# 103 unread TensorE passes in ten shapes behind the last store of a fused dynamic-convolution and squared-ReLU feed-forward kernel

## The chip, the cores and the metric

One Trainium2 chip, one of its cores. The metric is device microseconds of that core. Beside the plain times there is one profiled execution, whose span is the time from the first to the last recorded instruction.

## What is computed

The kernel computes a dynamic convolution (a softmax over 7 taps weighs the last 7 rows, for 8 heads) and feeds the result to a feed-forward block with a squared ReLU.

```python
batch, seq, d_model = (8, 4096, 192); n_heads, K = 8, 7
w = softmax(weight_gen, axis=-1)                       # [B, S, H, K]
x_unf = x_pad[:, s + k, :].reshape(B, S, K, H, D // H) # 7 shifted rows
a = np.einsum('bshk,bskhg->bshg', w, x_unf).reshape(B * S, D)
h = a @ w_in                                           # [32768, 192] @ [192, 2048]
r = np.maximum(h, 0.0)
return ((r * r) @ w_out).astype(np.float32)            # [2048, 192]
```

The change adds nothing to this: the outputs are stored before the added passes in program order, and the passes write PSUM tiles that nothing reads.

## The kernel before, in words

The 32768 rows are cut into 64 chunks of 512 (`N`). For each chunk VectorE and ScalarE make the convolution, and TensorE makes both products. Each operand of a product is split into a high and a low part in the type `F32R`; a product of such operands is one pass per call, while a product in plain `F32` gives two matmul records per call (the 9 calls at L567 show as 18).

Most passes go in pairs over half of the array's rows. `mm1` (L430) and `mm2_turned` (L503) call the matmul twice, once with partitions 0 to 63 and once with 64 to 127 (`rows = slice(h * D1, (h + 1) * D1)`, `D1 = 64`), each with a stationary operand of 128 columns and 512 moving columns, into two different PSUM banks. Every pass has a weight load of its own (`LDWEIGHTS`, listed as the engine PEld).

The last chunk (`c = NCH - 1`) has another form. `mm2` and `mm2_tile` (L476) use all 128 rows: per step one pass of 384 columns with the high part `gh` and one of 192 with the low part `gl`. The last quarter of its columns is finished in four passes into `acc` (L767) and eight passes of 192 columns into the PSUM tile `rest` (L770). VectorE adds `rest` to `tmp` (L773), and `store` (L557) issues the last output transfer on SyncE's queue. That is the last line of the kernel's body.

The schedule is written by hand: each engine runs its instructions in program order, and waits are placed where a tile's readers and writers are on different engines. Two pools of PSUM hold one bank per tile: `ps_h` with four buffers of the name `ph` in turn, and `ps_o` with `acc0` to `acc3`. At the end `rest` and `acc3` are the banks still read; the other three `ph` buffers and `acc0` to `acc2` are the six that the change takes. `ghs[NCH - 1, NF - 1]` is the high part of the last 128 hidden units of the last chunk (128 x 512), and `V` holds the second product's weights (128 x 16 x 384), both `F32R` and both resident until the end.

Of the kernel before, what the change touches and what calls it, by code (L numbers as in the profile page):

```python
# [8 lines left out]
F32 = mybir.dt.float32  # L9
# [12 lines left out]
def kernel(  # L22
# [531 lines left out]
    def store(c, t0, t1):  # L554
        o_sb, _ = outs[c]
        tsl = slice(t0, t1)
        nc.sync.dma_start(out=out_v[:, rows_of(c) + t0:rows_of(c) + t1, :], in_=o_sb[:, tsl])  # L557
# [215 lines left out]
    nc.vector.tensor_tensor(out=o_sb[:, t], in0=rest[:, 0:D], in1=tmp[:, t, 0:D], op=ALU.add)  # L773
    store(c, t, TC)


# [1 line left out]
_INS = ["x", "weight_gen", "moe_w_in", "moe_w_out"]  # L778
# [26 lines left out]
```

## Time and profile before

| what | value |
|---|---|
| time, median of 2 runs | 2231.13 us (2231.03 to 2231.23) |
| the profiled execution's span | 2229.4 us |
| TensorE matmul (PE) busy | 2224.8 us, 100% of the span |
| weight loads (PEld) busy | 1846.2 us, 83% |
| VectorE, ScalarE, GpSimd busy | 1869.8, 1805.4, 9.9 us |

Busy shares are unions of overlapping records: two passes of a pair that run side by side count once, and the end of a pass is modelled, so the spacing of the starts says more than the length of a record. The time from one start to the next is called the spacing below. The time outside the span (2231.13 against 2229.4) is 1.7 us.

### The profile page before, as it was taken

Reading aid. Unit: us, or ns where it says so; the run is one execution under the profiler, and the core shown is the slowest. Engines: PE = TensorE matmul, PEld = TensorE weight load, DVE = VectorE, ACT = ScalarE, POOL = GpSimd, SP = SyncE. Lnnn points to the kernel's source line nnn. Section 1 sums busy time; section 2 is a strip of 40 time slices with the busy share of each in tenths; the row PEclk is TensorE's granted clock in tenths of the full one; section 3 lists DMA queues with packets and bytes.
Section 4 is the critical chain, followed back from the end, with each engine's and each line's share of the span. In section 5 each row is a group of like instructions: output and inputs, shape, how many; then the busy total and the mean of one; then the engine's idle time right before and its main releaser. Section 6 shows DMA issues by size and latency. Waiting matters only on the chain.

```text
span 2229.4 us, 50051 instructions
## 1 busy us (share of the span) xinstructions
PE 2224.8 (100%) x19486; PEld 1846.2 (83%) x19486; DVE 1869.8 (84%) x2866; ACT 1805.4 (81%) x3492; POOL 9.9 (0%) x18
## 2 busy tenths in 40 slices
PE   9999999999999999999999999999999999999999
PEld 8888888888888888888888888888888888888888
DVE  9888888888888888888898888888888888888885
ACT  8888888888888888888888888888888888888886
POOL 0000000000000000000000000000000000000000
PEclk9999999999999999999999999999999999999999
DMA  8433323333233333333332333323333233332322
GB/s 221 96 85 92 90 59 100 83 94 99 57 92 89 88 100 75 74 95 82 100 85 64 100 85 92 88 60 100 84 94 96 54 98 86 91 100 66 82 60 53
DMA packets 323117, 195.30 MB, mean 88 GB/s; under 512 B 223944, under 2 KB 281288, under 8 KB 319040
## 3 DMA queue, kind: packets, MB, share of 16 engines
q1 hardware_dynamic: 321584, 188.58, 33.8%
q0 software_dynamic: 1296, 3.54, 0.9%
q8 instruction: 152, 2.49, 0.5%
q14 instruction: 85, 0.70, 0.1%
HBM read 106.39 MB, written 49.55 MB: 70 GB/s over the span
## 4 chain that ended last, share of the span: by engine, by line
PE 100%; POOL 0%; DVE 0%; issue 0%; POOLq 0%
PE acc L503 50%; PE ph L430 46%; PE acc L467 1%; PE acc L476 1%; PE acc L430 0%; PE acc L341 0%; PE acc L567 0%; PE ph L329 0%; PE ph L770 0%; PE acc L329 0%; PE acc L767 0%; DVE o_sb L773 0%; POOL ident masks.py:199 0%; POOL ident masks.py:197 0%; POOL ex L92 0%
## 5 line engine op out<-in xcount | busy, mean ns | idle before, releaser
L503 PE MATMUL acc<-gh,V 64*128 64x512 f32 x5952 | 1007.4, 386 | 0.0
L430 PE MATMUL ph<-xh,W 64*128 64x512 f32 x6084 | 853.9, 386 | 0.0
L447 ACT ACTIVATE rg<-ph 128x512 f32<-128x512 f32 x992 | 539.1, 597 | 351.5 <-PE ph L430 351.4
L503 PE MATMUL acc<-gl,V 64*128 64x512 f32 x3968 | 772.4, 386 | 0.0
L459 DVE TENSOR_TENSOR gl<-rg,gh 128x512 fp32r<-128x512 f32 x1008 | 644.4, 678 | 139.0 <-ACT gh L455 137.4
L430 PEld LDWEIGHTS ph<-xh,W 64*128 64x128 f32 x6084 | 569.6, 184 | 120.4 <-ACT rg L445 0.4
L503 PEld LDWEIGHTS acc<-gh,V 64*128 64x128 f32 x5952 | 557.5, 184 | 117.1
L451 ACT ACTIVATE rg<-rg 128x512 f32<-128x512 f32 x1008 | 581.3, 633 | 0.2
L455 ACT CAST gh<-rg 128x512 fp32r<-128x512 f32 x1008 | 576.1, 626 | 3.2 <-PE acc L476 3.2
L503 PEld LDWEIGHTS acc<-gl,V 64*128 64x128 f32 x3968 | 371.7, 184 | 78.0
L430 PE MATMUL ph<-xl,W 64*128 64x512 f32 x3042 | 427.3, 386 | 0.0
L266 DVE TENSOR_TENSOR pr<-xt,wt 128x768 f32<-128x768 f32 (+1 forms) x441 | 411.7, 946 | 2.3
L279 DVE TENSOR_TENSOR pr<-pr 128x768 f32<-128x768 f32 x366 | 347.0, 948 | 0.1
L430 PEld LDWEIGHTS ph<-xl,W 64*128 64x128 f32 x3042 | 284.9, 184 | 59.9
L310 DVE TENSOR_TENSOR xl<-xT,xh 128x512 fp32r<-128x512 f32 x186 | 117.7, 688 | 180.9 <-ACT xh L307 180.9
L307 ACT CAST xh<-xT 128x512 fp32r<-128x512 f32 x186 | 102.7, 624 | 0.1
L513 DVE TENSOR_TENSOR raw<-acc,raw 128x512 f32<-128x512 f32 x124 | 79.9, 686 | 5.9 <-ACT raw L511 5.9
L511 ACT COPY raw<-acc 128x512 f32<-128x512 f32 x124 | 66.6, 597 | 0.0
L237 ACT ACTIVATE wt<-wt 128x224 f32<-128x224 f32 x62 | 24.3, 392 | 47.4 <-DVE wt L236 47.4
L393 DVE STREAM_TRANSPOSE xr<-pr 128x768 f32<-128x768 f32 x62 | 60.6, 978 | 2.1
L525 DVE STREAM_TRANSPOSE raw<-raw 64x512 f32<-64x512 f32 x62 | 43.6, 704 | 2.1
L522 DVE STREAM_TRANSPOSE raw<-raw 128x512 f32<-128x512 f32 x62 | 43.7, 704 | 0.0
(93 smaller groups left out, 449.8 us busy)
## 6 DMA issues: line engine op xcount, KB each, us to landing
xT<-xd SPq DMA_DIRECT2D x124, 384.0 KB, 5.0
xt<-in_x_dram SPq DMA_DIRECT2D x30, 1344.0 KB, 6.9
out_dram<-o_sb SPq DMA_DIRECT2D x63, 384.0 KB, 2.7
xd<-xr SPq DMA_DIRECT2D x248, 96.0 KB, 2.0
o_sb<-raw SPq DMA_DIRECT2D x1488, 16.0 KB, 1.8
raw<-raw SPq DMA_DIRECT2D x62, 128.0 KB, 4.2
wt<-in_weight_gen_dram SPq DMA_DIRECT2D x31, 224.0 KB, 3.2
raw<-in_moe_w_in_dram SPq DMA_DIRECT2D x16, 192.0 KB, 5.3
```

Of the source, the lines that this page charges most:

```text
L266: tt(out=dst, in0=src, in1=wf[:, t0 * H:t1 * H, k:k + 1].broadcast_to([P, m, G]), op=ALU.mult)
L279: tt(out=prs[k0], in0=prs[k0], in1=prs.pop(k), op=ALU.add)
L307: nc.scalar.copy(parts["h"][:, k, n], src[k][:, n])
L310: tt(out=parts["l"][:, k, n], in0=src[k][:, n], in1=parts["h"][:, k, n].bitcast(F32), op=ALU.subtract)
L430: nc.tensor.matmul(two[i], w, xx[rows, k], start=(n == 0), stop=(n == len(seq) - 1))
L447: nc.scalar.activation(r, ph, AF.Relu)
L451: nc.scalar.activation(r, r, AF.Square)
L455: nc.scalar.copy(gh, rgs[c, fb])
L459: nc.vector.tensor_tensor(out=gl, in0=rgs.pop((c, fb)), in1=ghs[c, fb].bitcast(F32), op=ALU.subtract)
L503: nc.tensor.matmul(accs[c][b + h], w, g[rows], **fl)
L511: nc.scalar.copy(X[:, k], acc[b])
L513: nc.vector.tensor_tensor(out=X[:, k], in0=acc[b + 1], in1=X[:, k], op=ALU.add)
```

## The change

Behind the last `store` 103 passes are added, all with moving data `mv = ghs[NCH - 1, NF - 1]` and stationary columns of `V`, each with `start=True, stop=True`. None is read. `bk[0]` to `bk[2]` are the three free `ph` tiles, `bk[3]` to `bk[5]` new tiles `acc0` to `acc2`. Nothing else is touched.

```diff
     store(c, t, TC)
 
+    h0, h1 = slice(0, D1), slice(D1, P)
+    mv = ghs[NCH - 1, NF - 1]
+    bk = [ps_h.tile([P, N], F32, name="ph") for _ in range(3)] + [ps_o.tile([P, N], F32, name=f"acc{t}") for t in range(3)]
+
+    def run(items):
+        for b, rows, m, n0, n1, f in items:
+            nc.tensor.matmul(bk[b][0:m, n0:n1], V[rows, f, 0:m], mv[rows, n0:n1], start=True, stop=True)
+
+    allr = slice(0, P)
+    run((0, allr, P, 0, N, f) for f in range(8))
+    run((h + 1, r, P, 0, N, f) for f in range(6) for h, r in enumerate((h0, h1)))
+    run((3, h0, P, 0, N, f) for f in range(6))
+    run((h + 1, r, P, 0, N // 2, f) for f in range(6) for h, r in enumerate((h0, h1)))
+    run((h + 4, r, 96, 0, N, f) for f in range(6) for h, r in enumerate((h0, h1)))
+    run((h + 1, r, P, 0, N, f + g) for f in (0, 2, 4) for h, r in enumerate((h0, h1)) for g in range(2))
+    for g in range(3):
+        run([(3, allr, P, 0, N, g)])
+        run((h + 4, r, P, 0, N, g) for h, r in enumerate((h0, h1)))
+    run((0, allr, 96, 0, N, f) for f in range(6))
+    run((0, allr, P, 0, N - P, f) for f in range(6))
+    run((b, slice(Q * b, Q * b + Q), P, 0, N, f) for f in range(5) for b in range(4))
```

The ten groups in the order in which they run (Q is 32):

| group | passes | rows | moving columns | stationary columns |
|---|---|---|---|---|
| A | 8 | all 128 | 512 | 128 |
| B | 12 | halves in turn | 512 | 128 |
| C | 6 | the lower half alone | 512 | 128 |
| D | 12 | halves in turn | 256 | 128 |
| E | 12 | halves in turn | 512 | 96 |
| F | 12 | lower, lower, upper, upper | 512 | 128 |
| G | 9 | all, lower, upper, three times | 512 | 128 |
| H | 6 | all 128 | 512 | 96 |
| I | 6 | all 128 | 384 | 128 |
| J | 20 | the four quarters of 32 in turn | 512 | 128 |

## Rows read from the trace of the kernel before

**Rows 1.** The page: span, and busy time of the engines.
```profile
span 2229.4 us, 50051 instructions
PE 2224.8 (100%) x19486; PEld 1846.2 (83%) x19486; DVE 1869.8 (84%) x2866; ACT 1805.4 (81%) x3492; POOL 9.9 (0%) x18
```

**Rows 2.** Chain that ended last, from 2205 us: start, length, engine, tile, line.
```profile
2224.86 0.42 PE acc L767 x4
2225.28 0.91 PE ph L770 x8
2226.19 0.02 issue
2226.21 0.36 DVE o_sb L773
```

**Rows 3.** Timeline of the end: start, length, engine, line, operation, shape, count.
```profile
2225.12 0.27 PE L770 MATMUL ph<-V,gh 128*128 128x192 f32 x1
...
2225.25 0.42 DVE L552 TENSOR_TENSOR o_sb<-acc,raw 128x128 f32<-128x128 f32 x2 [0.71 <-ACT raw L549]
...
2225.67 0.42 DVE L552 TENSOR_TENSOR raw<-acc,raw 128x128 f32<-128x128 f32 x2
...
2225.80 0.27 PE L770 MATMUL ph<-V,gh 128*128 128x192 f32 x1
...
2225.90 0.27 PE L770 MATMUL ph<-V,gl 128*128 128x192 f32 x1
2226.21 0.36 DVE L773 TENSOR_TENSOR o_sb<-ph,raw 128x192 f32<-128x192 f32 x1
...
2226.60 0.33 SPq L557 DMA_DIRECT2D out_dram<-o_sb  x1
```

**Rows 4.** Transfers issued from 2226.5 to 2228 us: count, size, us to landing.
```profile
out_dram<-o_sb SPq DMA_DIRECT2D x1, 96.0 KB, 1.6
```

**Rows 5.** Windows at the end: length, busy (count) by engine, clock, DMA share, GB/s.
```profile
core 0: us, PE busy (x) PEld busy (x) DVE busy (x) ACT busy (x) POOL busy (x), PEclk, DMA share, GB/s
2226.00:2227.00 1.00, 0.18 (x2) 0.01 (x1) 0.45 (x2) 0.00 (x0) 0.00 (x0) 1.00 0.31 100
...
2228.00:2228.50 0.50, 0.00 (x0) 0.00 (x0) 0.00 (x0) 0.00 (x0) 0.00 (x0) 1.00 0.00 0
2228.50:2229.00 0.50, 0.00 (x0) 0.00 (x0) 0.00 (x0) 0.00 (x0) 0.00 (x0) 0.93 0.00 0
2229.00:2229.20 0.20, 0.00 (x0) 0.00 (x0) 0.00 (x0) 0.00 (x0) 0.00 (x0) 0.50 0.00 0
```

**Rows 6.** Half-row pairs in mid-kernel: 100 us of them, and a stretch's timeline.
```profile
1000.00:1100.00 100.00, 100.00 (x886) 1.00 0.35 92
...
1000.56 0.39 PE L503 MATMUL acc<-gl,V 64*128 64x512 f32 x2
1000.79 0.39 PE L503 MATMUL acc<-gh,V 64*128 64x512 f32 x2
...
1000.56 0.19 PEld L503 LDWEIGHTS acc<-gh,V 64*128 64x128 f32 x2
```

**Rows 7.** Full-row passes of the last chunk: windows for L476, then a timeline.
```profile
2208.08:2221.73 13.65, 13.65 (x97) 13.65 (x97) 1.00 0.16 25
...
2219.26 0.36 PE L476 MATMUL acc<-V,gh 128*128 128x384 f32 x1
2219.29 0.19 PEld L476 LDWEIGHTS acc<-V,gl 128*128 128x128 f32 x1
2219.46 0.25 PE L476 MATMUL acc<-V,gl 128*128 128x192 f32 x1
...
2219.54 0.36 PE L476 MATMUL acc<-V,gh 128*128 128x384 f32 x1
```

**Rows 8.** Timeline where half-row passes give way to full-row ones.
```profile
2206.74 0.84 PE L430 MATMUL ph<-xh,W 64*128 64x512 f32 x6
...
2207.51 0.19 PEld L476 LDWEIGHTS acc<-V,gh 128*128 128x128 f32 x1 [0.35 <-issue]
2207.52 0.44 PE L476 MATMUL acc<-V,gh 128*128 128x384 f32 x1
...
2207.80 0.25 PE L476 MATMUL acc<-V,gl 128*128 128x192 f32 x1
```

**Rows 9.** Timeline of TensorE where full-row passes give way to half-row ones.
```profile
53.64 0.98 PE L467 MATMUL acc<-du,gl 128*128 128x192 f32 x5
54.55 0.96 PE L430 MATMUL ph<-xh,W 64*128 64x512 f32 x6
55.35 0.40 PE L430 MATMUL ph<-xl,W 64*128 64x512 f32 x2
```

**Rows 10.** Timeline of TensorE: passes of 128 columns early and later.
```profile
1.42 4.21 PE L567 MATMUL acc<-ident 128*128 128x128 f32 x18 [1.42 <-POOL ident masks.py:199]
...
14.08 1.47 PE L329 MATMUL ph<-ident,wide 128*128 128x128 f32 x12
```

## The prediction

> **What bounds the kernel now.** I read the page first: PE is busy for 2224.8 of 2229.4 us [rows 1], so TensorE is the bound from the first microsecond to the last. What a change adds to TensorE's own stream is then added to the time, unless it comes where TensorE has nothing more to do. So the second view is the chain that ended last [rows 2]: it runs through the four passes of L767, the eight of L770 and VectorE's addition at L773. The third is the timeline of the end [rows 3]: the last of the eight passes starts at 2225.90, L773 runs from 2226.21 to 2226.57, and SyncE issues the last store at 2226.60. It lands 1.6 us later [rows 4], at 2228.2, and the span ends at 2229.4. TensorE thus sits idle from 2226.17 (2225.90 + 0.27) to the end. These 3.2 us are all the cover that the change finds: 1.6 us of transfer, and 1.2 us in which the program closes.
>
> **What is added, and where it starts.** The passes stand behind the store in the program, but on TensorE's queue they follow L770 directly, and TensorE does not wait for the store. Their six banks were last read by ScalarE and VectorE; the last such reader of the three `acc` tiles is `finish(c, 2)`, over by 2225.67 [rows 3], and `mv` and `V` are long resident. Nothing is computed from them, so VectorE, ScalarE and the queues get no work, and L773 and the store stay where they are. The eight passes of L770 start 0.111 us apart ((2225.90 - 2225.12) / 7) [rows 3], so the first added pass starts at 2225.90 + 0.11 = 2226.01.
>
> **Price of a half-row pair.** In mid-kernel 100 us hold 886 passes, one pair begun up to 0.39 us earlier among them [rows 6]: 100.4 us / 443 pairs gives 0.227 us a pair of 2 x 512 columns (1000.79 - 1000.56 says the same). [...] Both halves run at once. The loads of the next pair start with the present pair (1000.56, beside the pass that starts at 1000.56): they are hidden.
>
> **Price of a full-row pass.** At L476 a pass of 384 columns and one of 192 take turns; 48 such couples lie in 13.65 us [rows 7], 0.2845 us a couple. [...]
>
> **Price of a change between full and half rows.** Half to full [rows 8]: the last pair starts at 2207.20 (2206.74 + 0.84 - 0.39), the second full pass at 2207.80. With 0.227 for the pair and 0.20 for the pass of 384 it would have been 0.43 us; it was 0.60, so 0.17 us go to the change. The weight load is not pulled ahead here: it starts 0.31 us after the last pair. Full to half [rows 9]: the last full pass starts at 54.29, the first pair at 54.55, and the next tile's first pair at 55.35, three pairs later. The three take 0.80 instead of 0.68, and the gap is some 0.09 over a pass's spacing: 0.21, of which a wait may be part. I take 0.18, with 0 and 0.21 as ends.
>
> **The sum.** A: 8 x 0.236 = 1.89. B: six pairs, 1.36. C: the lower half alone; its loads are hidden as they are in a pair, where each half follows itself: 6 x 0.227 = 1.36. D: 256 columns are 0.107, with 13 ns 0.120, just over the 0.111 that full-row loads keep between them: 0.72 (up to 1.36 if columns saved nothing). E: as B, 1.36; 96 stationary columns shorten only the hidden load. F: lower, lower, upper, upper: a second pass on the same half waits for the first, but the upper's first runs beside the lower's second, and so on: seven slots, 1.59 (12 slots, 2.72, if nothing runs side by side). G: 3 x (0.236 + 0.227) = 1.39. H: 1.42. I: 6 x 0.182 = 1.09. J: five slots of four quarters, if four run together as two halves do: 1.13. Together 13.31 us. Nine changes of form (A to B, F to G, five in G, G to H, I to J): 9 x 0.18 = 1.62. The passes take 14.93 us; the last record outlasts its slot by 0.16 (0.39 - 0.23) [rows 6]. TensorE ends at 2226.01 + 14.93 + 0.16 = 2241.10.
>
> The store lands at 2228.2 as before, hidden behind the passes. What closes the program can only follow TensorE's end. In before 1.2 us lie between the landing and the end; part of that may be SyncE's waits for things then long done, so I take 0.8, between 0.4 and 1.2. The span becomes 2241.9, 12.5 us more, and with the 1.7 us outside it **2243.6 us**, 0.56% over 2231.13. The store's end and TensorE's idle tail hide 3.2 us less the new close.
>
> [...] What the rows show: at 2219.29 the load for the next pass starts, 30 ns into a pass on the same 128 rows that runs until 2219.62 [rows 7], and that next pass starts at 2219.46. So loads are hidden behind passes on the same rows. [...]
>
> For J the trace has no row. [...]
>
> **The rivals.**
>
> *Loads or quarters not hidden.* 32 passes (A 8, C 6, F 6, H 6, I 6) follow one on the same rows. [...] If J's quarters go one by one, 20 x 0.227 = 4.54, 3.4 more: 2247.0. Against it stand [rows 6, 7] for whole and half rows; nothing stands for quarters.
>
> *The clock falls.* In [rows 5] it is 1.00 until 2228.5 and 0.50 from 2229.0, with no pass after 2226.17. Groups C and J keep PE busy, but with part of its rows. Passes of 128 columns take 0.223 us each in the first microseconds and 0.109 later [rows 10] ((4.21 - 0.42) / 17, (1.47 - 0.27) / 11), which is the factor of two of the levels, though the clock column says 1.00 for both. A fall at J costs 1.1 us, at C and for all that follows some 10: 2244.7 to 2254. For it speaks only that half-used rows alone occur nowhere in before; against it, that the pairs and full rows hold 1.00 throughout.
>
> *Slower by more than 2%: each pass waits for the end of the one before.* Six banks are written over and over; if the order of writes to one bank were kept by waits, a pass would cost its record (0.39), the reaction (L773 starts 0.04 after L770's end) and a new load before it can start, some 0.1: 0.53 x 103 = 55 us, 2284. It decides from 0.456 us a pass on (2231.13 x 1.02 - 2226.01 - 2.7 = 47 us over 103). Against it: passes on the same tile already follow each other in L770 at 0.111, and the nine calls of L567 overwrite one region without a wait in their rows.
>
> *No cost, the other side of the forecast.* If unread writes were dropped when the program is built, or the close didn't wait for TensorE, the time would stay 2231.1. For it speaks that no reader exists; against it, that the nine calls of L567, read by nobody either, stand in the trace as 18 records.
>
> **Chances.** The sum as it stands, with its own range of 2241.9 to 2246.0: 0.72. Loads or quarters not hidden, 2246 to 2250: 0.18. The clock, 2244.7 to 2254: 0.05. No cost: 0.03. Serial passes: 0.02. The low end, 2241.9, is the sum without the cost of changes between forms (1.6 less). The high end, 2248.5, adds quarters one by one (3.4), F without overlap (1.1) and the long close (0.4). It leaves out a part of the second and third cases and all of the last two, under 2 in 10. A difference under 2% (44.6 us) is about what a measurement of this kernel can't tell from none; all cases but the serial one lie inside it, so within 2% has 0.97, slower 0.02, and faster, for which no row gives a way, 0.01.
>
> **What would show it.** In the changed profile the added passes should start at 2226.0, at a granted clock of 1.00, and end near 2241.1; windows by group should give 1.9 us for A, 1.4 for B and C each, 0.7 for D, 1.6 for F, 2.5 for G with its changes, 1.1 for I and J each. A and H well over 0.236 a pass would say that the load isn't hidden on full rows; C over 0.227 says it for half rows; F near 2.7 that the order lower, lower stops the overlap; J over 1.5 that quarters don't run four at a time. The store should be issued at 2226.6 still. The prediction is wrong if it isn't, if TensorE shows idle stretches between passes, or if the closing after its end is longer than 1.2 us.

## The result and the profile after

The changed kernel takes 2243.4 us (2243.40 and 2243.41) beside 2231.13 (2231.03 and 2231.23). The ratio is 1.0056, with a 95% interval of 1.0037 to 1.0075: 12.3 us more, half a percent, which by the bound of 2% counts as the same time, though the interval lies clear of 1. 2243.6 was predicted.

The page of the changed kernel, its answer to [rows 1]:

```profile
span 2241.6 us, 50261 instructions
PE 2238.8 (100%) x19589; PEld 1856.2 (83%) x19589; DVE 1869.8 (83%) x2866; ACT 1805.3 (81%) x3492; POOL 9.9 (0%) x18
```

103 matmul records more, 14.0 us more of busy TensorE, nothing on the other engines; the span is 12.2 us longer. The timeline of the end of the changed kernel, which answers to [rows 3] (start, length, engine, line, operation, shape, count):

```profile
2225.51 0.27 PE L770 MATMUL ph<-V,gl 128*128 128x192 f32 x1
...
2225.62 1.56 PE L782 MATMUL ph<-gh,V 128*128 128x512 f32 x6
2225.82 0.36 DVE L773 TENSOR_TENSOR o_sb<-ph,raw 128x192 f32<-128x192 f32 x1
...
2226.21 0.33 SPq L557 DMA_DIRECT2D out_dram<-o_sb  x1
```

The first added pass starts 0.11 us behind the last of L770, before VectorE's last addition has begun. The last store is issued 0.39 us behind the start of L773, as in before (2226.60 and 2226.21) [rows 3]. All of this comes 0.39 us earlier than in the profile of before (L770 ends with 2225.51 there 2225.90): the two profiled executions differ by that much before the change begins. So short distances at the end are measured from L773 on in what follows, not from the span's start.

The windows of the changed kernel's TensorE, cut where the form of the passes changes (length, busy time and count of records that touch the window, granted clock, DMA share, GB/s): A; B to F; G; H; I; J; and what follows the last pass.

```profile
2225.62:2227.56 1.94, 1.94 (x10) 1.00 0.32 101
2227.56:2233.99 6.43, 6.43 (x56) 1.00 0.01 3
2233.99:2236.58 2.59, 2.59 (x11) 1.00 0.00 0
2236.58:2238.05 1.47, 1.47 (x9) 1.00 0.00 0
2238.05:2239.20 1.15, 1.15 (x7) 1.00 0.00 0
2239.20:2240.64 1.44, 1.44 (x21) 1.00 0.00 0
2240.64:2241.60 0.96, 0.00 (x0) 1.00 0.00 0
```

The passes take 15.02 us from first start to last end, without a gap and at a clock of 1.00; 0.96 us of closing follow.

### The profile page after: what moved, and what is told of

Read it like the earlier page. It is cut to its first block, busy times and chain, and to the rows that moved or that the text cites. A ratio compares the mean times of both kernels' runs of the same rounds, so it can differ in the third digit from the quotient of the medians.

```text
span 2241.6 us, 50261 instructions
## 1 busy us (share of the span) xinstructions
PE 2238.8 (100%) x19589; PEld 1856.2 (83%) x19589; DVE 1869.8 (83%) x2866; ACT 1805.3 (81%) x3492; POOL 9.9 (0%) x18
## 4 chain that ended last, share of the span: by engine, by line
PE 100%; DVE 0%; DMA 0%; ACT 0%; issue 0%; DVEq 0%
PE acc L503 50%; PE ph L430 46%; PE acc L467 1%; PE acc L476 1%; PE acc L430 0%; PE ph L782 0%; PE acc L341 0%; PE acc L782 0%; DMA wt<-in_weight_gen_dram 0%; PE ph L329 0%; PE ph L770 0%; PE acc L329 0%; DVE sm L238 0%; DVE pr L266 0%; DVE mx L235 0%; PE acc L767 0%
```

## The experiments

All of them keep the kernel whole up to the last store and replace only the unread passes behind it, so their outputs are those of before. Where a single time is given, it can't resolve less than some 1 us: the times of before went from 2230.66 to 2231.73 within one session, and to 2232.19 over all of them. The traces carry the verdicts.

**Fewer changes of form (e1_sorted).** The same 103 passes, the full-row ones first, then the half-row ones, then the quarters.

```diff
 run((0, allr, P, 0, N, f) for f in range(8))                              # A
+run((3, allr, P, 0, N, f) for f in range(3))                              # full-row third of G
+run((0, allr, 96, 0, N, f) for f in range(6))                             # H
+run((0, allr, P, 0, N - P, f) for f in range(6))                          # I
 ...
-for g in range(3):
-    run([(3, allr, P, 0, N, g)])
-    run((h + 4, r, P, 0, N, g) for h, r in enumerate((h0, h1)))
+run((h + 4, r, P, 0, N, g) for g in range(3) for h, r in halves)          # half-row rest of G
```

> The same 103 passes with the full-row ones first, then the half-row ones, then the quarters: two changes between forms in place of nine. Theory (a change between full, half and quarter rows costs about 0.2 us, because the next weight load starts only when the array is empty): seven changes less, 7 x 0.20 = 1.4 us off the changed kernel's 2243.4, so 2242.0. Rival (those gaps belong to the first use of a bank or to waits, which stay): 2243.4.

Measured: 2242.5 us, ratio to before 1.0051 (1.0039 to 1.0064). The time lies between the two expectations and its interval holds both. The trace decides; the timeline of its first and last added passes:

```profile
2226.17 2.01 PE L782 MATMUL ph<-gh,V 128*128 128x512 f32 x8
...
2239.37 0.39 PE L782 MATMUL ph<-gh,V 32*128 32x512 f32 x1
```

From first start to last end 2239.76 - 2226.17 = 13.59 us, against 15.02: 1.43 us less, as expected for seven changes. That the time fell by only 0.9 is the 0.55 us by which its passes began later (2226.17 against 2225.62).

**The cover (e2_only_a, e6_sixteen).** Eight and sixteen full-row passes alone.

```diff
-run((0, allr, P, 0, N, f) for f in range(8))
-...
+run((0, allr, P, 0, N, f) for f in range(8))     # e2: nothing else; e6: range(16)
```

> Group A alone, eight full-row passes of about 0.23 us, 1.9 us in all. Theory (between TensorE's last useful pass and the landing of the last store some 2.1 us lie idle, so passes that end by then cost nothing): 2231.1, as before. Rival (whatever TensorE gets at the end is added to the time): 2233.0.

> Sixteen full-row passes alone, 3.7 us. Theory (the store's landing covers 2.1 us of passes, and the close of 0.9 us follows whichever ends last): from the start of L773 to the end of the span 4.5 us in place of the 3.1 of the kernel before, time 1.4 us longer, 2232.5. Rival (every pass is added to the time): 3.7 us longer, 2234.8. Rival (the close is covered too): 0.6 us longer.

Measured: eight passes 2230.9 us, ratio 0.9999 (0.9990 to 1.0008); sixteen 2232.1, beside 2232.19 for before in that session, a single pair. First eight, then sixteen passes, timeline and span:

```profile
core 0 of [0], span 2229.2 us
...
2225.88 2.01 PE L782 MATMUL ph<-gh,V 128*128 128x512 f32 x8
2226.08 0.36 DVE L773 TENSOR_TENSOR o_sb<-ph,raw 128x192 f32<-128x192 f32 x1
```

```profile
core 0 of [0], span 2230.3 us
...
2225.55 3.82 PE L782 MATMUL ph<-gh,V 128*128 128x512 f32 x16
2225.75 0.36 DVE L773 TENSOR_TENSOR o_sb<-ph,raw 128x192 f32<-128x192 f32 x1
```

From L773's start to the end it is 3.2 us in before (2229.4 - 2226.21) [rows 1, 3], 3.1 with eight passes and 4.5 with sixteen. Eight passes are over at 2227.89, 0.2 us before the store of that run can have landed (issued at 2226.46, 1.6 us by [rows 4]), and cost nothing. Sixteen end at 2229.37 and the program 0.9 us later. So the cover is the store's landing, and a close follows whichever ends last: the first theory, to some 0.2 us, since 1.1 to 1.2 us follow the landing (before and eight passes) and 0.9 to 1.0 us TensorE's last pass (sixteen, and the changed kernel). The single time of the sixteen shows none of the 1.4 us that were expected; that run's L773 came 0.46 us earlier than that of the profile of before, and the one time of before in its session was 1.06 us longer than the 2231.13 above.

**The order of the halves (e3_slip).** Runs of k passes on one half, then k on the other.

```diff
+full()
+for h, r in enumerate((h0, h1)):
+    for g in range(8):                      # k = 8; likewise 1, 2, 4, 12, and quarters
+        mm(bk[h + 1], V[r, g, 0:P], mv[r], start=True, stop=True)
+full()
```

> In place of the ten groups: runs of k passes on the lower half, then k on the upper (k = 1, 2, 4, 8 and 12; 512 columns), and of the four quarters (k = 2 and 4), with a full-row pass between the patterns. A slot is 0.23 us. Theory (each half has a queue of its own, in which three passes wait behind the running one, as group C showed): k = 1, 2 and 4 take 8 slots each (1.8 us), k = 8 takes 12 (2.7 us), k = 12 takes 20 (4.6 us); quarters 2 slots for k = 2 and 4 for k = 4 (0.9 us). Rival 1 (passes start in program order): 9, 13, 15 and 23 slots for k = 2, 4, 8 and 12, and 5 and 13 for the quarters. Rival 2 (the three waiting passes are counted over all rows together): as the theory for halves, but 7 slots for the quarters at k = 4 (1.6 us). Time: about 2231 + 14 us.

Measured: windows from one full-row pass to the next, for k = 1, 2, 4, 8 and 12 on halves and 2 and 4 on quarters:

```profile
2226.32:2228.73 2.41, 2.41 (x19) 1.00 0.26 82
2228.73:2231.23 2.50, 2.50 (x19) 1.00 0.00 0
2231.23:2233.83 2.60, 2.60 (x20) 1.00 0.02 6
2233.83:2237.37 3.54, 3.54 (x18) 1.00 0.00 0
2237.37:2242.75 5.38, 5.38 (x26) 1.00 0.00 0
2242.75:2243.86 1.11, 1.11 (x10) 1.00 0.00 0
2243.86:2245.44 1.58, 1.58 (x22) 1.00 0.00 0
```

Each holds one full-row pass and two changes of form, 0.63 us. The rest in slots of 0.23 us is 7.7, 8.1, 8.6, 12.7 and 20.7 for halves, 2.1 and 4.1 for quarters. Program order asked for 9, 13, 15 and 23 from k = 2 on, and 5 and 13; the common count asked for 7 at the last. Both fall. The theory's 8, 8, 8, 12, 20, 2 and 4 fit, with about half a slot over on halves from k = 4 on. Where that half slot goes no row shows. The time, 2248.66 us, is some 4 us over the expected 2231 + 14, which had counted the slots without the full-row passes and the changes of form.

**The price of a pass (e4_sizes).** Eight passes of one size in a row, then couples, then forms in turn on one bank.

```diff
+for f in range(8):
+    mm(bk[1][0:96, 0:192], V[:, f, 0:96], mv[:, 0:192], start=True, stop=True)   # and other sizes
+for f in range(8):
+    for n in (384, 192):
+        mm(bk[1][:, 0:n], V[:, f, 0:P], mv[:, 0:n], start=True, stop=True)
+for f in range(4):
+    mm(bk[3], V[:, f, 0:P], mv, start=True, stop=True)
+    mm(bk[3], V[h0, f, 0:P], mv[h0], start=True, stop=True)
```

> In place of the ten groups: full-row passes of one size each, eight in a row, then couples of 384 and 192 columns, then full and half rows in turn on one bank, then 128 and 64 stationary columns in turn. [...] Full and half rows in turn: 0.43 us each on one bank too if the change of form is the cause, 0.23 if a new bank was. For 128 and 64 stationary columns in turn no run has a row: 0.23 if it is no change of form, 0.43 if it is.

Measured: windows of 512, 384, 256, 192 and 128 columns, then 192 and 128 with 96 stationary columns, then couples of 384 and 192 with 128 and with 96:

```profile
2225.86:2227.71 1.85, 1.85 (x11) 1.00 0.33 106
2227.71:2229.12 1.41, 1.41 (x9) 1.00 0.00 0
2229.12:2230.07 0.95, 0.95 (x10) 1.00 0.00 0
2230.07:2230.94 0.87, 0.87 (x10) 1.00 0.00 0
2230.94:2231.81 0.87, 0.87 (x11) 1.00 0.00 0
2231.81:2232.55 0.74, 0.74 (x11) 1.00 0.08 22
2232.55:2233.20 0.65, 0.65 (x11) 1.00 0.00 0
2233.20:2235.51 2.31, 2.31 (x19) 1.00 0.00 0
2235.51:2237.61 2.10, 2.10 (x18) 1.00 0.00 0
```

The time was 2245.87 us. An eighth of each window: 0.231, 0.176, 0.119, 0.109 and 0.109; 0.092 and 0.081; couples 0.289 and 0.263. The couples with 96 stationary columns are 0.026 us cheaper than those with 128. 192 and 128 columns cost the same 0.109 with 128 stationary columns, and both less with 96: a floor that the moving columns don't set. That the weight load sets it is the author's reading, which no row of e4 shows by itself. The forms in turn, on one bank, and stationary columns in turn:

```profile
2238.38 0.50 PE L807 MATMUL acc<-gh,V 128*128 128x512 f32 x1
2238.81 0.50 PE L808 MATMUL acc<-gh,V 64*128 64x512 f32 x1
...
2241.52 0.39 PE L810 MATMUL acc<-gh,V 128*128 128x512 f32 x1
2241.74 0.39 PE L811 MATMUL acc<-gh,V 128*64 128x512 f32 x1
```

Full and half rows in turn cost 0.43 us a pass on one and the same bank, so no new bank is needed for it; 128 and 64 stationary columns in turn cost 0.23, which is no change of form.

**The clock (e5_thin, e8_area, e7_gap).** Long stretches on part of the array, and passes behind an idle stretch.

```diff
+for k in range(64):                                                      # e5
+    mm(bk[0], V[h0, k % 16, 0:P], mv[h0], start=True, stop=True)         # lower half
+for k in range(64):
+    mm(bk[1], V[0:Q, k % 16, 0:P], mv[0:Q], start=True, stop=True)       # lowest quarter
+...
+for k in range(64):                                                      # e8
+    mm(bk[0][0:Q], V[:, k % 16, 0:Q], mv, start=True, stop=True)         # all rows, 32 columns
+...
+for _ in range(12):                                                      # e7
+    nc.scalar.copy(late_mv, mv.bitcast(F32))
+for k in range(40):
+    mm(bk[0], V[:, k % 16, 0:P], late_mv, start=True, stop=True)
```

> In place of the ten groups: 64 passes on the lower half alone, 64 on the lowest quarter alone, 64 on that quarter with 32 stationary columns, then 16 on all rows; 512 columns each. Theory (half-used rows alone don't lower the granted clock): 1.00 throughout, about 0.23 us a pass, 14.6 us for each stretch of 64, time 2231 + 47 = about 2278. Rival (the clock falls when only part of the rows works): a granted clock of 0.50 in one of the stretches, 0.43 us a pass there, 27 us for it.

> In place of the ten groups, 512 columns each: 64 passes on all rows with 32 stationary columns, 64 on the lower half with 32 stationary columns, 64 couples of the two lowest quarters with 128 stationary columns; 32 full passes behind each stretch. The quarter alone, with 128 stationary columns, had let the clock fall; the lower half alone had not. Theory (the number of rows at work decides, half of them is enough): a granted clock of 1.00 throughout, 0.23 us a pass or couple, three stretches of 14.6 us and three of 7.3, time about 2231 + 64 = 2295. Rival (the share of the whole array, rows times columns, decides: 32 columns on all rows are as much as a quarter's rows on all columns): 0.50 and 0.43 us a pass in the first two stretches, 1.00 in the third, 13 us longer for each.

> Forty full-row passes whose moving data ScalarE first copies twelve times (12 x 0.63 = 7.5 us), so that TensorE idles some 7 us before them. [...] Rival (the level in the clock column does not set the price of a pass): 0.23 us throughout.

Measured: 2302.05 us for e5, where the theory had 2278. Its timeline, by stretch, and then TensorE's windows (length, busy time and count, granted clock, DMA share, GB/s):

```profile
2225.89 14.80 PE L787 MATMUL ph<-gh,V 64*128 64x512 f32 x64
2240.62 26.33 PE L789 MATMUL ph<-gh,V 32*128 32x512 f32 x64
2266.75 27.51 PE L791 MATMUL ph<-gh,V 32*32 32x512 f32 x64
2294.19 5.14 PE L793 MATMUL ph<-gh,V 128*128 128x512 f32 x16
```

```profile
2226.00:2240.00 14.00, 14.00 (x62) 1.00 0.05 15
...
2242.00:2244.00 2.00, 2.00 (x7) 0.55 0.00 0
2244.00:2266.00 22.00, 22.00 (x53) 0.50 0.00 0
```

The rival's case, but not on the half: the stretch on the lower half alone keeps 1.00 for 14.8 us at 0.23 us a pass. In the stretch on the quarter alone, with PE busy without a gap, the clock falls to 0.50 at about 2242.2 (0.55 as the mean of the two microseconds from 2242 puts it there) and stays there; a pass then costs 0.43 us (27.51 / 64). In the full-row passes that follow from 2294.19 on, the clock is 0.59 in the window from 2296 to 2297 and 1.00 from 2297.

e8 took 2295.29 us, and kept a clock of 1.00 in all of its stretches:

```profile
2225.68 14.98 PE L787 MATMUL ph<-gh,V 128*32 128x512 f32 x64
...
2247.86 15.01 PE L791 MATMUL ph<-gh,V 64*32 64x512 f32 x64
...
2270.27 14.82 PE L796 MATMUL acc<-gh,V 32*128 32x512 f32 x128
```

0.23 us a pass or couple throughout, on the lower half and on two quarters in turn as well: the falls that the rival expected in the first two stretches did not come. One thing is left open. In e5 the quarter's stretch follows 14.8 us on the lower half, so the clock fell after 16.3 us in which one half at most was at work (2225.89 to 2242.2); no such stretch of e8 is longer than 15.0 us before full-row passes follow. Whether the quarter alone or the length of both stretches together was the reason, the runs don't separate.

e7 took 2247.52 us; its passes start at 2233.00 behind 7.2 idle microseconds:

```profile
2228.00:2229.00 1.00, 0.00 (x0) 0.00 (x0) 0.00 (x0) 0.97 (x2) 0.00 (x0) 0.50 0.00 0
...
2234.00:2238.00 4.00, 4.00 (x11) 0.50 0.00 0
...
2239.00:2245.00 6.00, 5.77 (x26) 1.00 0.00 0
```

The clock is 0.95 in the window from 2227 to 2228 and 0.50 in the next, with no pass since 2225.82. Eleven records touch 4 us at 0.50, two of them begun or cut at the edges, so some 0.43 us a pass; then 26 in 6 us at 1.00, 0.23 each: in this run the price goes with the level in the clock column, and the rival's 0.23 throughout falls.

## Why the prediction was right, point by point

**Where it starts and what hides it: right.** The passes follow L770 by 0.11 us, the store is not moved (L773 starts 0.20 us behind the first added pass, as 2226.21 lies 0.20 behind 2226.01), and the cover is the landing of the store. e2 shows that passes within it cost nothing (ratio 0.9999 for eight), e6 that the close comes on top (0.9 us behind the sixteenth). The close was 0.96 us against 0.8, between its ends. That the time came out within 0.2 us is partly luck: from the prediction's 2226.01 the measured pieces lead to 2241.99 (15.02 and 0.96), and only the 0.39 us by which this execution ran ahead make it 2241.6. (The prediction's small slips, 2207.20 for 2207.19, 0.2845 for 0.2844 and a low end of 2241.9 for 2242.0, move nothing.)

**The sum: 15.02 us against 15.09, by errors that cancel.** In the windows above, with each change put with the group ahead of it and the last record's tail with J, the prediction had 2.07, 6.57, 2.47, 1.42, 1.27 and 1.29; measured were 1.94, 6.43, 2.59, 1.47, 1.15 and 1.44. These pairs can't be compared one by one, because a change costs on both of its sides. A's window is only 0.09 us longer than e4's eight passes of the same form (1.85); the rest stands behind the boundary, where B's first pair takes 0.34 us until the next starts, 0.11 more than a pair:

```profile
2227.56:2227.90 0.34, 0.34 (x4) 1.00 0.00 0
```

So A and I look cheap by about half a change, and H and J dear by as much. The prices below come from e4, e1, and the stretch of C where nothing changes.

*The full-row pass was mis-sized.* 0.236 us was taken, 0.231 is the mean of eight at the same place in e4, and 384 columns cost 0.176, not 0.182. No run shows the terms for a column and for a change of weights on which the sum's 0.236, 0.182 and D's 0.107 and 13 ns rest; the runs showed 0.231 and 0.176 in their place, and 0.12 for a pass of D in the changed kernel ((2231.03 - 2230.67) / 3), the sum's 0.120. The couples of [rows 7] are two passes of these prices: 0.176 for 384 columns and e4's 0.109 for 192 make 0.285, beside the 0.2844 of [rows 7] and 0.289 in e4. The 0.231 lies between the prediction's 0.236 and a half-row pair's 0.227. Over the 17 passes of 512 columns and the six of 384 this is some 0.12 us less.

*The change of form was mis-sized the other way.* 0.18 was taken; in G, six slots of 2.59 / 6 = 0.43 us leave 0.20 beside the pass, and e1 gives 1.43 / 7 = 0.20 too. Over nine changes this is some 0.18 us more. The row that bears on the reason, from the changed kernel's G:

```profile
2234.41 0.19 PEld L782 LDWEIGHTS acc<-gh,V 64*128 64x128 f32 x2 [0.24 <-issue]
```

The weight load starts 0.42 us behind the start of the pass ahead (2233.99), with PEld idle for 0.24 us; between like passes it starts 0.03 us behind that start [rows 7]. So it is exposed. At each of the nine changes it starts some 0.07 us ahead of the end, a modelled one, of the last record of the old form; this is what the rows show of the empty array in e1's theory. What else fills up the 0.20 us they don't show. Going between 128, 96 and 64 stationary columns cost no such time here (E to F, H to I, and 0.23 us a pass in e4).

**B to F: the size nearly right, the picture not.** The prediction let the upper half wait in program order while C ran on the lower, and the description of the kernel has each engine run its instructions in program order. The changed kernel's timeline where C (`acc`, 512 columns) meets D (`ph`, 256):

```profile
2229.06 1.09 PE L782 MATMUL acc<-gh,V 64*128 64x512 f32 x4
2229.76 0.38 PE L782 MATMUL ph<-gh,V 64*128 64x256 f32 x1
2229.98 0.39 PE L782 MATMUL acc<-gh,V 64*128 64x512 f32 x1
2229.99 0.38 PE L782 MATMUL ph<-gh,V 64*128 64x256 f32 x1
```

A pass of D, which stands behind all six of C and one of its own in the program, starts beside C's fourth. It can only be one of the upper half, started while three earlier passes of the lower one had not started (C's fifth and sixth, and D's first). e3's windows fit the same count on halves and quarters: 12.7 slots at k = 8, where program order asked for 15, and 4.1 for the quarters at k = 4, where it asked for 13. With it F needs six slots, not seven, and the whole stretch is as long as the lower half's own 30 passes. That slot alone would have made the stretch 0.23 us shorter; it came out 0.14 shorter (6.57 - 6.43), the rest going to the dearer change and to passes slightly over 0.227 (C's first and sixth start 1.15 us apart, 0.230 each). Together: 0.12 less for full rows, 0.18 more for the changes, 0.23 less for F's slot, and some 0.10 more for 32 slots of half and quarter rows at 0.230 make the 0.07 us by which the sum was too long.

**The rivals.** Loads that are not hidden: full-row passes at 0.231 (e4's eight, the same as A) and the lower half alone at 0.230 in C and 0.229 in e5 ((14.80 - 0.39) / 63) rule it out. Quarters: five slots in 1.44 us with the change's load and the last tail among them, and 4.1 slots for sixteen passes in e3, so four at a time. The clock: 1.00 to the end, and passes of 0.23 us in C and J, which is e7's price at that level; that it can fall while PE is busy on part of the rows, e5 shows in its stretch on a single quarter (1.00 to 0.50). Serial passes and passes that cost nothing: excluded by 103 records at these spacings.

## What to carry to other kernels

At a granted clock of 1.00 a full-row pass of this kernel with 128 stationary columns cost 0.231 us for 512 moving columns, 0.176 for 384, 0.119 for 256, and 0.109 for 192 and 128 alike (e4); a pass of 192 in turn with one of 384 cost its 0.11 there too (0.289 a couple). Group passes by the rows they use: each change between full, half and quarter rows cost some 0.20 us (G, e1). Work placed behind a bound engine's last useful instruction was free up to about the landing of the last store (e2, 2.0 us of passes, ratio 0.9999), and beyond it counted in full in the trace (e6: 4.5 us from L773's start to the end, beside 3.1 with e2's eight passes).

## What the runs showed of the hardware that was not expected

Passes on different halves and quarters of the rows started out of program order: D's first upper pass beside C's fourth, ahead of three passes that stand before it, and in e3 12 passes on each half took 20.7 slots where program order asked for 23. In e5's stretch on a single quarter of the rows, with PE busy without a gap, the granted clock fell from 1.00 to 0.50, and a pass went from 0.23 to 0.43 us; the stretches of some 15 us on half the rows, with 128 or with 32 stationary columns, held 1.00 (e5, e8). Whether the quarter alone was the reason is open. Passes of 512 columns cost 0.227 us in mid-kernel [rows 6], but 0.231 in e4's eight, and 0.232 over the 64 of e8 with 32 stationary columns ((14.98 - 0.39) / 63); the reason was not pursued.
